# First FFN chunk in plain float32, smaller early chunks, weights divided one chunk later, clears issued behind the raw weights

## The chip, the core and the metric

The kernel runs on one core of a Trainium2 chip. A core has a matrix engine (TensorE, PE in the profile; its weight loads are PEld), three engines for elementwise work (VectorE or DVE, ScalarE or ACT, GpSimd or POOL), an engine that issues most transfers (SyncE or SP), and 16 DMA engines. Each engine works through its own instruction stream in order and waits for others by semaphores. Matrix results land in PSUM, eight banks of 512 float32 in each of 128 partitions; everything else lies in SBUF or in device memory. The metric is device time in microseconds, the median of several runs.

## The reference

Three layers follow each other: attention that keeps the 32 largest scores of each row, a feed-forward layer (FFN) with a squared ReLU, and a mixture of 8 experts of which each token uses two.

```python
scores = scale * np.matmul(q, k.transpose(0, 1, 3, 2))          # 4 x 8 x 576 x 576, head size 64
kth = np.partition(scores, -top_k, axis=-1)[..., -top_k:-top_k + 1]   # top_k = 32
scores = np.where(scores >= kth, scores, -1000000000.0)
attn = np.exp(scores - np.max(scores, axis=-1, keepdims=True))
x = (attn / (attn.sum(-1, keepdims=True) + 1e-09)) @ v          # 2304 tokens x 512
h = np.maximum(x @ w_in, 0.0); x = h * h @ w_out                # 512 -> 2048 -> 512
logits = x @ w_gate + np.log1p(np.exp(x @ w_noise)) * noise     # two largest of 8 experts
out[mask] += top2_w * (np.maximum(x[mask] @ w1[e], 0.0) @ w2[e])  # 512 -> 1024 -> 512
```

The FFN's weights arrive as 64-bit floats, the rest as float32.

## The kernel before

**Tokens.** The 2304 tokens make 18 tiles of 128. Each of the four batches has 576 queries: four full tiles and 64 left over, and the leftovers of two batches share a tile. Attention goes by units. A full unit is one tile and one pair of heads (64 of them); a left unit is 64 leftover queries and one pair of heads (16). `LEFT_AFTER` says after which tile of its batch the left units stand. In a unit TensorE multiplies queries and keys (line 394), VectorE searches the 32 largest scores (lines 407 to 448; two searches in a full unit, one in a left one, 144 in all, each with two instructions of line 435), GpSimd and ScalarE mask and exponentiate (lines 460 to 466), TensorE transposes (lines 477, 500, 501) and multiplies with the values (line 514), and `finish` divides by the row sum and splits the result (lines 486 to 492).

**Split matmuls.** Where a matmul must be as good as float32, both operands are split into a high part that the engine's fast format holds exactly and a low remainder, and three fast matmuls (high-high, high-low, low-high) are summed. The keys and queries, the FFN (lines 319 to 321 and 305 to 307) and the experts work so. Products with the values, transposes and routing logits (line 188) are plain float32.

**FFN chunks.** `CHUNKS` cuts the 18 tiles into six chunks of three. A chunk's `ffn` is a generator of small pieces. It becomes available when all units of its tiles are done. For each of 16 slices f of the hidden layer it loads the divided weights `wi` and `wo` (512 KB each, two buffers) from the scratch tensor `wsc`, does four first steps (three matmuls each, as wide as the chunk), squares the ReLU and splits it (lines 325 to 329), and does one second step a tile for the slice before (three matmuls of 512 columns). The sums of up to three tiles stand in the three banks of `ps_acc` until line 176 moves them out; then `route` picks the experts and scatters the rows to the slots `xs`.

**Conversions.** `convert` turns the 64-bit weights into divided float32, 32 pieces in all: it loads a raw piece (512 KB, three buffers), ScalarE and VectorE build the high word (lines 153, 155, 156, the scratch in PSUM for the first 14 pieces and in SBUF after), ScalarE and GpSimd add the low word (157, 158), then both split the value (161, 162), and it is written to `wsc` (163). 

**Clears.** `zero_fill` writes empty rows to the experts' slots (40 transfers of 258 KB) and to the output (18 of 256 KB).

**Order.** The program is written unit by unit. Between parts of a unit `step` takes FFN and routing pieces from the background, as many as a rate (`FIRST_RATE`, `RATE`, in estimated us a unit, less for left units) allows, and `side` takes conversions (three a unit) and, from unit 9 of the list on, clears. Each side work gets a priority, and a scheduler sets the final order on every engine by priority and its own estimate of time. Two kinds of instructions keep a fixed order among themselves by a token: the searches, and the last chunk with the early experts. After attention the rest of the FFN runs, three experts start on their first 384 slots while the last chunk finishes, and then the experts follow one another.

## Time and profile before

| | |
|---|---|
| median of 3 runs | 1365.13 us (1363.53 to 1368.26) |
| the profiled execution | 1361.43 us |
| its span, first to last instruction | 1359.7 us |
| TensorE busy | 1240.0 us, 91% |
| VectorE busy | 889.0 us, 65% |
| ScalarE busy | 862.3 us, 63% |
| GpSimd busy | 773.3 us, 57% |
| mean granted TensorE clock | 0.971 |

The shares are averages over stages with different limits, so they are to be read stage by stage. Matmuls are pipelined and their printed lengths overlap: how fast TensorE goes is read from start to start. A matmul whose operands are both plain float32 appears as two instructions. In the chain of waits a piece is the work that the end of the program was waiting for at that moment.

### The profile page before, as it was taken

What the parts mean: (1) busy time and instruction counts of PE and PEld (TensorE: products, weight loads), DVE (VectorE), ACT (ScalarE), POOL (GpSimd) and SP (SyncE); (2) the same over time, 40 slices, a digit from 0 to 9 for tenths busy, and PEclk for the clock granted to TensorE, in tenths of its full rate; (3) what the DMA queues carried; (4) which work ended last, traced back from release to release, by engine and by line L of the source; (5) the groups of instructions that cost most, each with busy time, mean ns of one, the idle gap of its engine ahead of it and who ended that gap; (6) DMA issues with size and microseconds to landing.
All of it is one profiled execution on the core that took longest, in us unless ns stands there. A gap on an engine that the chain in (4) does not pass through costs nothing.

```text
span 1359.7 us, 25767 instructions
## 1 busy us (share of the span) xinstructions
PE 1240.0 (91%) x7937; PEld 1083.3 (80%) x7937; DVE 889.0 (65%) x4531; ACT 862.3 (63%) x1849; POOL 773.3 (57%) x1239
## 2 busy tenths in 40 slices
PE   3666689889999999899999998999999999999997
PEld 2554478778887888688878887889999899899876
DVE  7999979898777888998698101255544444444554
ACT  6988888898788878988797443543433323333343
POOL 5869999867875757777656536233441331513232
PEclk9787699999999999999999999999999999999999
DMA  9996688734764356166415768645653443434464
GB/s 321 362 359 232 207 298 303 257 122 136 253 215 163 122 178 226 44 198 220 153 57 176 234 245 272 221 147 194 202 165 122 134 148 124 150 114 146 137 202 139
DMA packets 86387, 261.65 MB, mean 192 GB/s; under 512 B 10844, under 2 KB 10972, under 8 KB 86240
## 3 DMA queue, kind: packets, MB, share of 16 engines
q1 hardware_dynamic: 76960, 231.51, 51.6%
q0 software_dynamic: 9280, 28.40, 5.7%
q8 instruction: 65, 1.06, 0.3%
q14 instruction: 82, 0.67, 0.2%
HBM read 209.90 MB, written 52.06 MB: 193 GB/s over the span
## 4 chain that ended last, share of the span: by engine, by line
PE 67%; DVE 9%; DMA 7%; ACT 4%; POOL 3%; issue 2%; SPq 0%; POOLq 0%; DVEq 0%; ACTq 0%
PE ph L643 5%; PE ph L644 5%; PE ph L645 5%; PE acc L624 5%; PE acc L626 5%; PE acc L625 5%; PE pa L514 4%; PE acc L305 4%; PE acc L306 4%; PE acc L307 4%; PE ps L394 4%; PE pf L319 4%; PE pf L321 3%; PE pf L320 3%; PE pa L477 3%; DVE w L411 2%
## 5 line engine op out<-in xcount | busy, mean ns | idle before, releaser
L407 DVE MAX8 m<-sb 128x8 f32<-128x115 f32 (+1 forms) x720 | 190.4, 265 | 69.5 <-ACT sb L396 64.5
L465 POOL TENSOR_TENSOR sb<-sb,w 128x576 f32<-128x576 f32 x144 | 205.7, 1430 | 46.4 <-ACT w L464 44.0
L411 DVE MATCH_REPLACE8 w<-m,sb 128x115 f32<-128x115 f32 (+1 forms) x720 | 186.9, 262 | 0.0
L665 POOL DMA_INDIRECT out<-y,info x40 | 45.9, 1148 | 241.2 <-DVE y L664 223.5
L649 ACT ACTIVATE ht<-ph 128x384 fp32r<-128x384 f32 (+1 forms) x128 | 55.8, 436 | 194.5 <-PE ph L645 194.5
L394 PE MATMUL ps<-K,qt 128*128 128x288 f32 (+2 forms) x640 | 130.6, 333 | 43.5 <-ACT sb L396 22.3
L650 DVE SCALAR_TENSOR_TENSOR ht<-ph,ht 128x384 fp32r<-128x384 f32 (+1 forms) x128 | 62.6, 489 | 162.3 <-ACT ht L649 162.2
L643 PE MATMUL ph<-xe,wi 128*128 128x256 f32 (+1 forms) x512 | 159.4, 311 | 1.7 <-ACT wi L636 1.2
L645 PE MATMUL ph<-xe,wi 128*128 128x256 f32 (+1 forms) x512 | 158.6, 310 | 0.2 <-DVE wi L637 0.2
L644 PE MATMUL ph<-xe,wi 128*128 128x256 f32 (+1 forms) x512 | 158.7, 310 | 0.0
L394 PEld LDWEIGHTS ps<-K,qt 128*128 128x128 f32 x640 | 103.4, 204 | 59.8 <-ACT sb L396 31.7
L329 POOL TENSOR_TENSOR gt<-r,gt 128x384 fp32r<-128x384 f32 x96 | 98.1, 1023 | 73.5 <-ACT gt L328 60.1
L466 ACT ACTIVATE sb<-sb,keep 128x576 f32<-128x576 f32 x144 | 112.2, 779 | 27.9 <-POOL sb L465 27.0
L624 PE MATMUL acc<-wo,ht 128*128 128x512 f32 x320 | 125.9, 397 | 0.7 <-DVE y L664 0.7
L625 PE MATMUL acc<-wo,ht 128*128 128x512 f32 x320 | 125.2, 395 | 0.0
L319 PE MATMUL pf<-xT,wi 128*128 128x384 f32 x320 | 111.9, 350 | 10.2 <-ACT xT L491 4.7
L305 PE MATMUL acc<-wo,gt 128*128 128x512 f32 x288 | 113.7, 409 | 6.3 <-DMA wo<-wsc 5.1
L464 ACT ACTIVATE w<-sb,keep 128x576 f32<-128x576 f32 x144 | 111.4, 775 | 11.7 <-POOL keep L460 11.0
L435 DVE MAX8 m<-w 128x8 f32<-128x288 f32 x288 | 115.7, 442 | 0.1
L477 PE MATMUL pa<-ident,sb 128*128 128x128 f32 x576 | 96.8, 293 | 19.1 <-ACT sb L466 10.3
L320 PE MATMUL pf<-xT,wi 128*128 128x384 f32 x320 | 110.7, 346 | 3.5 <-POOL xT L492 3.4
L306 PE MATMUL acc<-wo,gt 128*128 128x512 f32 x288 | 111.8, 402 | 0.0
(203 smaller groups left out, 3440.5 us busy)
## 6 DMA issues: line engine op xcount, KB each, us to landing
wi<-wsc SPq DMA_DIRECT2D x96, 512.0 KB, 4.7
wo<-wsc SPq DMA_DIRECT2D x96, 512.0 KB, 4.8
raww<-in_exp SPq DMA_DIRECT2D x88, 512.0 KB, 3.7
raw<-in_ffn SPq DMA_DIRECT2D x32, 512.0 KB, 6.0
wsc<-csp SPq DMA_DIRECT2D x32, 512.0 KB, 4.5
xs<-xr SPq DMA_DIRECT2D x40, 258.0 KB, 7.2
mr<-xs SPq DMA_DIRECT2D x40, 258.0 KB, 3.1
qn<-in_q SPq DMA_DIRECT2D x40, 256.0 KB, 4.2
```

The costliest lines, as they stand in the source:

```text
L305: nc.tensor.matmul(acc[tt], gt[:, 0, sl], wo[:, 0, :], start=(f == 0), stop=False)
L306: nc.tensor.matmul(acc[tt], gt[:, 0, sl], wo[:, 1, :], start=False, stop=False)
L319: nc.tensor.matmul(ph[:, 0:n], wi[:, 0, sl], xT[:, 0, c, 0:n], start=(c == 0), stop=False)
L394: nc.tensor.matmul(ps[:, n, 0:w], st, kt[:, at:at + w], start=(i == 0), stop=(i == len(pairs) - 1))
L407: in_turn(nc.vector.max(parts[i][1], sb[:, parts[i][0]]))
L411: in_turn(nc.vector.match_replace(out=w[:, sl], in_to_replace=top, in_values=sb[:, sl], imm_value=NEG))
L465: nc.gpsimd.tensor_tensor(sb, sb, w, op=ALU.subtract)
L624: queued(nc.tensor.matmul(acc[t], hs[i][:, 0, sl], wo[:, 0, :], start=(f == 0), stop=False))
L625: queued(nc.tensor.matmul(acc[t], hs[i][:, 0, sl], wo[:, 1, :], start=False, stop=False))
L643: queued(nc.tensor.matmul(ph[:, 0:n], wi[:, 0, sl], xe[i][:, 0, c, :], start=(c == 0), stop=False))
L644: queued(nc.tensor.matmul(ph[:, 0:n], wi[:, 0, sl], xe[i][:, 1, c, :], start=False, stop=False))
L645: queued(nc.tensor.matmul(ph[:, 0:n], wi[:, 1, sl], xe[i][:, 0, c, :], start=False, stop=(c == NC - 1)))
```

## The change

- `CHUNKS` is now 2, 2, 2, 3, 3, 3, 3. The left units of the first batch stand behind its sixteen full units.
- Chunk 0 (two tiles) is computed with plain float32 matmuls, one where three stood; `finish` writes its input without a split, and the squared ReLU is not split either.
- A conversion ends with the whole value, written to a new scratch tensor `whole` (256 KB a piece). It no longer splits. Raw pieces and converted ones have four buffers each.
- Chunk 1 loads both whole pieces of a slice at once, divides them (ScalarE makes the high parts, GpSimd the low part of `wi`, VectorE that of `wo`), writes them to `wsc` and uses them. The later chunks load from `wsc` as before.
- Raw loads and clears share an issue-order token, so that no clear goes ahead of a raw load that is written earlier in the program.
- The rate of background work is worked out for each chunk from its pieces and the units until the next but one chunk is due, instead of two constants.

```diff
-CHUNKS = [3, 3, 3, 3, 3, 3]
-LEFT_AFTER = [3, 2, 0, 2]
+CHUNKS = [2, 2, 2, 3, 3, 3, 3]
+LEFT_AFTER = [4, 2, 0, 2]
...
+    def queue_turn(inst):
+        tc.stamp_issue_order_token(inst.ins, "loads")
...
-                nc.sync.dma_start(xs[e * NT + t * P:e * NT + (t + 1) * P, :], fill)
+                queue_turn(nc.sync.dma_start(xs[e * NT + t * P:e * NT + (t + 1) * P, :], fill))
...
-        nc.sync.dma_start(raw, w_ffn[f, which])
+        queue_turn(nc.sync.dma_start(raw, w_ffn[f, which]))
...
-        val = a.bitcast(F32)
-        sp = vpool.tile([P, 2, n], F32R, name="csp", bufs=2 if keep is not None else 1)
-        nc.scalar.activation(sp[:, 0, :], val, AF.Copy)
-        nc.gpsimd.tensor_tensor(sp[:, 1, :], val, sp[:, 0, :].bitcast(F32), op=ALU.subtract)
-        nc.sync.dma_start(wsc[f][:, which], sp.bitcast(F32))
+        nc.sync.dma_start(whole[f][:, which], a.bitcast(F32))
...
+        plain, divide = t0 == 0, t0 == CHUNKS[0]
...
+                if plain:
+                    nc.tensor.matmul(acc[tt], gt[:, 0, sl].bitcast(F32), wo[:, 0, :].bitcast(F32),
+                                     start=(f == 0), stop=(f == NF - 1))
...
+            if plain:
+                for i, w in enumerate((wi, wo)):
+                    nc.sync.dma_start(w[:, 0, :].bitcast(F32), whole[f][:, i])
+            elif divide:
+                raw = vpools[0].tile([P, 2 * DM], U32, name="raw", bufs=4 if keep is not None else 2).bitcast(F32)
+                nc.sync.dma_start(raw, whole[f].rearrange("p a d -> p (a d)"))
+                for i, (w, eng) in enumerate(((wi, nc.gpsimd), (wo, nc.vector))):
+                    part = raw[:, i * DM:(i + 1) * DM]
+                    nc.scalar.activation(w[:, 0, :], part, AF.Copy)
+                    eng.tensor_tensor(w[:, 1, :], part, w[:, 0, :].bitcast(F32), op=ALU.subtract)
+                    nc.sync.dma_start(wsc[f][:, i], w.bitcast(F32))
...
+                if plain:
+                    nc.tensor.matmul(ph[:, 0:n], wi[:, 0, sl].bitcast(F32), xT[:, 0, c, 0:n].bitcast(F32),
+                                     start=(c == 0), stop=(c == NC - 1))
...
+        rates.append(pieces(nt, i == 0) / sum(weight[done_at[i] + 1:until] + [1.0]))
...
-        return (FIRST_RATE if state["chunk"] == 0 else RATE) * (weight[i] if i < NU else 1.0)
+        return rates[state["chunk"]] * weight[i]
```

How the built program's order changes is shown at three places. First the transfer queue (SP) in the early program. `raw` is a raw weight piece, `xs` an empty slot block (a clear), `qn` queries. Before, around the fourth raw load:

```order
L136 DMA xs<-xr 128x516 x5
L147 DMA raw<-in_ffn 128x1024
L136 DMA xs<-xr 128x516 x4
L147 DMA raw<-in_ffn 128x1024
L136 DMA xs<-xr 128x516 x2
L163 DMA wsc<-csp 128x1024
L136 DMA xs<-xr 128x516
L163 DMA wsc<-csp 128x1024
L136 DMA xs<-xr 128x516 x2
L147 DMA raw<-in_ffn 128x1024
L136 DMA xs<-xr 128x516 x5
```

And in the changed program, from the 30th raw load on:

```order
L149 DMA raw<-in_ffn 128x1024
L138 DMA xs<-xr 128x516 x5
L161 DMA whole<-ca 128x512
L149 DMA raw<-in_ffn 128x1024
L406 DMA qn<-in_q 128x512
L161 DMA whole<-ca 128x512
L149 DMA raw<-in_ffn 128x1024
L138 DMA xs<-xr 128x516 x10
L161 DMA whole<-ca 128x512 x2
L138 DMA xs<-xr 128x516 x5
L161 DMA whole<-ca 128x512
L138 DMA xs<-xr 128x516 x6
```

Clears stood between the raw loads; now nearly all stand behind them, and the output's clears follow.

Next VectorE between two searches, marked by the pairs `MAX m<-w` at lines 435 and 462. `low` and `m` are search work; `ca` is a conversion's value. Before, from the 12th search to the 13th:

```order
L435 MAX m<-w 128x8 x2
L407 MAX m<-sb 128x8
L438 TENSOR_SCALAR low<-m 128x5x11
L411 MATCH_REPLACE w<-m,sb 128x116
L443 MAX low_868<-low 128x8
L407 MAX m<-sb 128x8
L446 MATCH_REPLACE low<-low_868,low 128x5x11
L411 MATCH_REPLACE w<-m,sb 128x115
L443 MAX low_868<-low 128x8
L407 MAX m<-sb 128x8
L446 MATCH_REPLACE low<-low_868,low 128x5x11
L411 MATCH_REPLACE w<-m,sb 128x115
```

And in the changed program, from the 12th search on:

```order
L462 MAX m<-w 128x8 x2
L434 MAX m<-sb 128x8
L158 SCALAR_TENSOR_TENSOR ca<-raw,ca 128x512
L157 TENSOR_SCALAR ca<-ca 128x512
L465 TENSOR_SCALAR low<-m 128x5x11
L438 MATCH_REPLACE w<-m,sb 128x116
L499 RECIPROCAL sm<-sm 128x2
L158 SCALAR_TENSOR_TENSOR ca<-raw,ca 128x512
L470 MAX low_823<-low 128x8
L434 MAX m<-sb 128x8
L157 TENSOR_SCALAR ca<-ca 128x512
L473 MATCH_REPLACE low<-low_823,low 128x5x11
```

Where a search stood alone, the steps of several conversions stand within it; sixteen searches into the program thirty conversions have been placed, against six before.

Last TensorE around the 11th unit, whose value matmuls are `pa<-pt,vt`. `pf` and `acc` are FFN results, the rest is attention. Before:

```order
L514 MATMUL pa<-pt,vt 64x128 x8
L477 MATMUL pa<-ident,sb 128x128 x8
L319 MATMUL pf<-xT,wi 128x384
L500 MATMUL pa<-ident,sb 128x128
L501 MATMUL pa<-ident,rb 128x128
L320 MATMUL pf<-xT,wi 128x384
L321 MATMUL pf<-xT,wi 128x384
L394 MATMUL ps<-K_120,qt 128x288 x4
L514 MATMUL pa<-t_1928,vt 64x128 x2
L514 MATMUL pa<-pt,vt 64x128 x8
```

And in the changed program:

```order
L545 MATMUL pa<-pt,vt 64x128 x8
L504 MATMUL pa<-ident,sb 128x128 x4
L338 MATMUL pf<-xT,wi 128x256 x4
L504 MATMUL pa<-ident,sb 128x128 x4
L531 MATMUL pa<-ident,sb 128x128
L532 MATMUL pa<-ident,rb 128x128
L338 MATMUL pf<-xT,wi 128x256 x4
L421 MATMUL ps<-K_258,qt 128x288 x4
L545 MATMUL pa<-t_1934,vt 64x128 x2
L545 MATMUL pa<-pt,vt 64x128 x8
```

The first single steps of chunk 0 stood there; now whole slices of the plain chunk stand there. By the counts of the whole order, TensorE had 64 first and 48 second steps (of three matmuls) ahead of unit 28's value matmuls, 312 and 231 ahead of unit 80's, and 72 and 57 after. Now it has the whole plain chunk with 52 and 22 two-tile steps ahead of unit 28, 300 first steps (128 of them two tiles wide) and 193 second steps ahead of unit 80, and 84 and 63 after.

## Rows read from the trace of the kernel before

**Rows 1.** Stretches, core 0: engines' busy us (instructions), clock, DMA share, GB/s

```profile
0.00:98.00 98.00, 54.04 (x315) 41.94 (x316) 88.19 (x527) 77.38 (x152) 69.41 (x101) 0.88 1.01 354
98.00:306.00 208.00, 165.96 (x1125) 138.23 (x1125) 192.79 (x1077) 179.47 (x397) 186.76 (x210) 0.89 0.69 236
306.00:781.00 475.00, 459.44 (x3361) 402.11 (x3358) 368.89 (x2484) 387.29 (x876) 328.29 (x522) 1.00 0.51 170
540.00:600.00 60.00, 52.89 (x406) 45.06 (x405) 57.26 (x394) 55.04 (x125) 44.53 (x76) 0.97 0.30 97
781.00:884.00 103.00, 95.41 (x506) 83.54 (x506) 13.26 (x41) 45.24 (x89) 41.92 (x99) 0.98 0.73 245
884.00:1360.00 476.00, 465.18 (x2639) 417.44 (x2637) 225.87 (x408) 172.95 (x336) 146.97 (x310) 0.99 0.47 151
```

**Rows 2.** Chain of waits, searches: start, us, engine, tile, line, count

```profile
290.86 0.72 DVE m L435 x2
294.68 0.73 DVE m L435 x2
298.71 0.72 DVE m L435 x2
```

**Rows 3.** Groups of instructions: busy us, mean ns, idle before and releaser

```profile
L637 DVE TENSOR_TENSOR wo<-raww,wo 128x512 fp32r<-128x512 f32 x88 | 60.7, 690 | 26.1 <-ACT wo L636 24.9
L162 POOL TENSOR_TENSOR csp<-ca,csp 128x512 fp32r<-128x512 f32 x32 | 42.2, 1321 | 2.9 <-ACT csp L161 2.6 <-POOL keep L460 0.3
L158 POOL TENSOR_TENSOR ca<-ca,raw 128x512 uint32<-128x512 uint32 x32 | 41.6, 1301 | 5.5 <-issue 2.7 <-POOL xT L492 0.7 <-POOL keep L460 0.7
L156 DVE SCALAR_TENSOR_TENSOR ca<-raw,ca 128x512 uint32<-128x512 uint32 x18 | 22.3, 1241 | 0.2
L155 DVE TENSOR_SCALAR ca<-ca 128x512 uint32<-128x512 uint32 x18 | 16.4, 909 | 6.9 <-ACT ca L153 6.9
L155 DVE TENSOR_SCALAR acc<-acc 128x512 uint32<-128x512 uint32 x14 | 9.6, 688 | 0.0
L156 DVE SCALAR_TENSOR_TENSOR ca<-raw,acc 128x512 uint32<-128x512 uint32 x14 | 9.4, 673 | 0.0
```

**Rows 4.** Timeline, TensorE: start, us; the value matmuls of units 8, 28, 80

```profile
98.30 0.54 PE L514 MATMUL pa<-t,vt 128*64 128x128 f32 x4
...
305.65 0.44 PE L514 MATMUL pa<-t,vt 128*64 128x128 f32 x4 [1.25 <-ACT t L503]
...
779.52 0.44 PE L514 MATMUL pa<-t,vt 128*64 128x128 f32 x4
```

**Rows 5.** Line 176: the moves out of PSUM of all chunks' sums

```profile
L176 ACT COPY xr<-acc x18: 569/592/618, 286.5 to 879.5; 128x512 f32<-128x512 f32 x18
```

**Rows 6.** Timeline, TensorE: neighbours of 384, 512 and 256 columns

```profile
809.00 0.34 PE L321 MATMUL ph<-xT,wi 128*128 128x384 f32 x1
809.17 0.34 PE L319 MATMUL ph<-xT,wi 128*128 128x384 f32 x1
...
811.23 0.39 PE L305 MATMUL acc<-wo,gt 128*128 128x512 f32 x1
811.46 0.40 PE L306 MATMUL acc<-wo,gt 128*128 128x512 f32 x1
...
1004.53 0.28 PE L643 MATMUL ph<-xe,wi 128*128 128x256 f32 x1
1004.65 0.28 PE L644 MATMUL ph<-xe,wi 128*128 128x256 f32 x1
```

**Rows 7.** Chain of waits: value matmuls, scores, plain float32 matmuls of routing

```profile
332.25 1.24 PE pa L514 x20
334.25 1.29 PE ps L394 x8
...
803.37 1.85 PE acc L188 x16
807.63 0.98 PE acc L188 x8
```

More of the change, by code (lines that the diff above doesn't have):

```diff
@@ L81, in attention_ffn_moe @@
     tag = "" if keep is not None else "x"
+    whole = [nc.dram_tensor(f"whole{tag}{f}", (P, 2, DM), F32, kind="Internal").ap() for f in range(NF)]
     wsc = [nc.dram_tensor(f"wsc{tag}{f}", (P, 2, 2, DM), F32, kind="Internal").ap() for f in range(NF)]
@@ L145, in convert @@
         n = DM
-        raw = vpool.tile([P, 2 * n], U32, name="raw", bufs=3 if keep is not None else 2)
-        nc.sync.dma_start(raw, w_ffn[f, which])
+        raw = vpool.tile([P, 2 * n], U32, name="raw", bufs=4 if keep is not None else 2)
+        queue_turn(nc.sync.dma_start(raw, w_ffn[f, which]))
         pair = raw.rearrange("p (j t) -> p j t", t=2)
         lo_w, hi_w = pair[:, :, 0], pair[:, :, 1]
-        a = vpool.tile([P, n], U32, name="ca", bufs=2)
+        a = vpool.tile([P, n], U32, name="ca", bufs=4 if keep is not None else 2)
         high = ps_acc.tile([P, DM], F32, name="acc") if 2 * f + which < IN_PSUM else a.bitcast(F32)
@@ L296, in attention_ffn_moe @@
     after, mpools = [], []
+    vpools = []
     def ffn(t0, nt, xT):
@@ L326, in ffn @@
             gt = fpool.tile([P, 2, CH], F32R, name="gt")
[L327 to L329 removed]
+            if plain:
+                nc.scalar.activation(gt[:, 0, 0:n].bitcast(F32), r[:, 0:n], AF.Square)
+            else:
+                nc.scalar.activation(r[:, 0:n], r[:, 0:n], AF.Square)
+                nc.scalar.activation(gt[:, 0, 0:n], r[:, 0:n], AF.Copy)
+                nc.gpsimd.tensor_tensor(gt[:, 1, 0:n], r[:, 0:n], gt[:, 0, 0:n].bitcast(F32), op=ALU.subtract)
             yield True, 0.163 * nt
@@ L480, in transpose4, with finish @@
         return t
-    def finish(av, rt, dst, j, off, n):
+    def finish(av, rt, dst, j, off, n, plain):
+        if plain:
+            with tc.high_priority(SOON):
+                nc.vector.tensor_tensor(dst[:, 0, j, off:off + n].bitcast(F32), av[:, 0:n], rt, op=ALU.mult)
+            return
         x = apool.tile([P, P], F32, name="x", bufs=4)
@@ L675, in attention_ffn_moe, with pieces @@
     state = {"safe": True, "due": 0.0, "chunk": 0, "routed": 0}
-    def pieces(nt):
-        return NF * (NC * nt * 0.163 + nt * 0.65)
+    def pieces(nt, plain):
+        return NF * nt * (NC * (0.2 if plain else 0.163) + (0.8 if plain else 0.65))
     def step(n):
@@ L735, in attention_ffn_moe @@
                     units.append((b, NFULL * P, False, j, tiles.index((b - b % 2, None))))
+        if LEFT_AFTER[b] == NFULL:
+            units += [(b, NFULL * P, False, j, tiles.index((b - b % 2, None))) for j in range(H // 2)]
     NU = len(units)
@@ L780, in close @@
                     nc.gpsimd.tensor_copy(dsts[ch][:, :, :, (tt - t0) * P:(tt - t0 + 1) * P], lefts[tt])
-            background.append([ffn(t0, nt, dsts[ch]), pieces(nt)])
+            background.append([ffn(t0, nt, dsts[ch]), pieces(nt, ch == 0)])
+    rates = []
+    for i, (t0, nt) in enumerate(chunks):
+        until = done_at[i + 1] if i + 1 < len(chunks) else NU
+        rates.append(pieces(nt, i == 0) / sum(weight[done_at[i] + 1:until] + [1.0]))
     def rate(i):
-        return (FIRST_RATE if state["chunk"] == 0 else RATE) * (weight[i] if i < NU else 1.0)
+        return rates[state["chunk"]] * weight[i]
     q_split(0)
```

22 lines of the change are left out of this document (12 added, 10 removed).

## Prediction

> **What bounds the kernel now.** I read the stretches of the span first, one line per stage [rows 1]. In the first 306 us VectorE is the busy engine (88.2 of 98 us, then 192.8 of 208) and TensorE is not: 166 of 208 us by a busy count that includes matmul latency, at a granted clock of 0.88 to 0.89 of 2.4 GHz, so part of the time at 1.2. From 306 to 781 us, the rest of attention, this turns round: TensorE is busy 459.4 of 475 us, VectorE 368.9. From 781 to 884 us TensorE does FFN that attention left over, and from 884 us the experts, which the change does not touch. So time is saved only by matmul work moved forward into TensorE's early idle time, and an added matmul costs its full length unless it falls there.
>
> Then the prices. A search (one of 144, two in a full unit, one in a left unit) costs VectorE 4.0 us where nothing else holds it: its L435 pairs start 3.8 and 4.0 us apart [rows 2]. A conversion costs it 0.69 + 0.67 = 1.36 us with PSUM scratch (the first 14) and 0.91 + 1.24 = 2.15 us with SBUF scratch (the other 18), GpSimd 1.30 + 1.32 = 2.62 us [rows 3]. The last matmul group of unit 8 starts at 98.3 us, of unit 28 at 305.7, of unit 80 at 779.5 [rows 4]; I use these three as milestones. Chunk 0's sums leave PSUM at 286.5 us [rows 5], close to unit 28. TensorE's steps go by start to start, not by the length printed: 0.176 us for 384 columns (two at 0.17, rounded; a run of twelve gives 0.176), 0.234 for 512, 0.118 for 256 [rows 6]. A float32 matmul is two passes of 0.109 us for 128 columns, from (1.85 - 0.98)/8 [rows 7]. A first step (three matmuls of one slice) is thus 0.527 us for three tiles and 0.354 for two, a second step (three matmuls of 512 columns) 0.703. A full unit's own TensorE work is 1.29 for scores, ten transposes at 0.109 and 1.24 for values, 3.6 us [rows 7]; a left unit's I estimate at 3.0.
>
> **The change, part by part.** *TensorE, in all.* One FFN tile in three split matmuls takes 16 x (12 x 0.176 / 3 + 3 x 0.234) = 22.5 us. In plain float32 it takes 16 x (4 x 2 x 0.109 + 8 x 0.109) = 27.9 us. Chunk 0 has two tiles: 55.8 instead of 45.0, so TensorE has 11 us more to do. Two-tile chunks cost nothing more, as 0.118 is two thirds of 0.176. Where these 11 us land decides the case, and the order of the built program says how much FFN stands before each unit. Before unit 28 stood chunk 0, 67.5 us; now 55.8 + 52 x 0.354 (first steps) + 22 x 0.703 (second steps) = 89.7. Between units 28 and 80 stood 248 x 0.527 + 183 x 0.703 = 259; now 76 x 0.354 + 172 x 0.527 + 171 x 0.703 = 238. After unit 80 stood 72 x 0.527 + 57 x 0.703 = 78; now 84 and 63, 88.6. So: **+22, -21.6, +10.5 us.**
>
> *To unit 8.* Six conversions stood before its sixteenth search, now thirty do. VectorE therefore does 8 x 1.36 + 16 x 2.15 = 45 us more before that point, and nothing hides it, since VectorE is the bound there (88 of 98 us). Unit 8 goes from 98 to 143 us. At PSUM prices for all 24 it would be 33 us more, 131 us; both ends are kept. TensorE has some 30 us of work in this time, eight units at 3.6 and a first step or two, so it idles about 113 us, against 68 before. The clears no longer stand ahead of the raw loads, so I add no stall for those.
>
> *Units 9 to 28.* VectorE: 36 searches x 4.0, two conversions (4 us), and eleven of the sixteen new wo subtractions of chunk 1 at 0.69 [rows 3], 8 us: 156 us. TensorE: 16 x 3.6 + 4 x 3.0 + 89.7 + 3 for routing = 162 us. They do not overlap perfectly. In units 13 to 20 the program gives TensorE 68 us against 48 for VectorE, because four of them are left units and two steps of chunk 0 stand in each; in the other twelve units VectorE's 108 us is longer. That makes 176 us. In the same units VectorE lost 14 us before (208 us, for 194 of searches and conversions); GpSimd, busy 187 of 208, had a part in that and is relieved, so I add half, 7 us. Unit 28 comes at 143 + 183 = 326 instead of 306: **+20 us**. The low end is 131 + 162 = 293 (-13), the high end 143 + 176 + 14 = 333 (+27). So the early start fills TensorE's idle time of this stage, after the front loading has made about as much in the stage before.
>
> *Units 29 to 80.* TensorE is the bound here and has 21.6 us less. VectorE's total, 92 x 4.0 + 3.5 = 372 of 474 us, is far from it. But in units 29 to 36 and 45 to 48 the program now leaves so little FFN that searches set the pace for a few us. I take **-19 us**. It is -22 if nothing is lost, and -9 if half these units lose 5% as 540 to 600 us does, where VectorE sets the pace and 57.3 of 60 us are busy [rows 1].
>
> *After unit 80.* **+10.5 us**, on the path: TensorE is busy 95.4 of 103 us, and the stretch ends with the last chunk's routing. If the 7.6 idle us absorb most of it, +3; if two more weight loads are waited for, +13.
>
> *At nothing:* ScalarE's and GpSimd's savings in chunk 0 (no gt split, no x split) and the division moved from conversion to chunk 1. ScalarE is busy 179 of 208 us, and its copies keep their number. If ScalarE became late in units 21 to 28, where two copies a step stand beside the searches, it would cost up to 8 us, which the high end covers.
>
> **Sum.** +20 - 19 + 10.5 = +11.5 on the profiled execution's 1361.4 us: 1372.9. The median of the runs shown is 3.7 above that execution, so about **1376 us** by the median.
>
> **A rule against a row.** L156 takes 0.67 us where one operand lies in PSUM and 1.24 where both lie in SBUF [rows 3], while GpSimd was busy almost without pause. The Trainium skill, SBUF — State Buffer, section Who interferes with whom, says that a VectorE instruction with two SBUF inputs and a GpSimd instruction that reads SBUF exclude each other, one fully blocking. By that rule the 18 late conversions get cheaper as GpSimd's part of a conversion halves. The rows agree with the rule as far as the two forms differ.
>
> **Rivals.** *Cheaper conversions: faster.* If halving GpSimd's 2.62 us per conversion takes the SBUF form down to 1.36 on VectorE, unit 8 comes at 131, and if the two engines then mesh in units 9 to 28, unit 28 at 293: -13 - 22 + 10.5 = -24.5, or 1341. Half of it (unit 28 at 303) gives 1354. It decides from unit 28 at about 311, where the sum is -4. For it: 1.24 against 0.67 in the same line. Against it: the searches between need the same GpSimd, and the two-input wo subtractions come on top. Chance 0.23.
>
> *Clears before chunk 0: slower still.* The 58 clears, 15 MB, now go out together after the last raw load. At the 354 GB/s of the first 98 us they need 42 us. In the program 38 stand ahead of the weight load of chunk 0's third step. If that is late by 15 us at unit 10, TensorE waits with units 11 and 12 queued behind it: 1390. For it: loads and clears share one queue. Against it: the first clears go while the last conversions run. Chance 0.15.
>
> *Gains and losses cancel.* Unit 28 at 315 and the leftover partly absorbed: within 0.3%, 1365. Chance 0.20. That bound of 0.3% is about what a measurement of this kernel can tell from no change.
>
> **How the numbers follow.** My forecast, slower by 5 to 20 us, has 0.42; with the clears' case, slower holds 0.57, same 0.20, faster 0.23. The likeliest time is 1376. The range goes from 1352, which leaves out the faster rival's better half, to 1393, the clears' case with a little more: together the ends leave out about 0.2.
>
> **What would show it.** Right: unit 8 near 143 us, with TensorE idle in more than two thirds of the time until then; unit 28 near 326; from there to unit 80 some 455 us instead of 474; first-chunk sums out of PSUM near 225; about 10 us more between unit 80 and the experts. Wrong: L158 (the old L156) near 0.7 us in its SBUF form, or unit 28 before 311, speaks for the faster rival; TensorE waiting for wi or wo from whole around units 10 to 12 speaks for the clears. If the experts' stretch is not 476 us again, something I have not seen is at work.

## The result, and the profile after

The changed kernel takes 1375.0 us (median of 11 runs, 1370.6 to 1376.8), the kernel before beside it 1365.1 us (11 runs, 1362.7 to 1369.6). The ratio is 1.0059 with a 95% interval of 1.0044 to 1.0074: slower by 0.6%, outside the 0.3% that the prediction called no change. The profiled execution took 1376.78 us with a span of 1375.0, that of before 1361.43 with 1359.7. So the two traces lie 15.3 us apart and the medians 9.9; the traces tell where time went, the medians how much of it is usual.

The milestones that answer to [rows 4], the value matmuls of units 8, 28 and 80, from the timeline of TensorE after the change (start, us, engine, line, operation):

```profile
132.57 0.70 PE L545 MATMUL pa<-t,vt 128*64 128x128 f32 x4
...
321.72 0.44 PE L545 MATMUL pa<-t,vt 128*64 128x128 f32 x4
...
781.24 0.44 PE L545 MATMUL pa<-t,vt 128*64 128x128 f32 x4
```

The stretches between them, and the experts after; then two slices of 20 us. Columns as in [rows 1]: length, busy us of PE, PEld, DVE, ACT and POOL with instruction counts, granted TensorE clock, DMA share, GB/s.

```profile
0.00:132.57 132.57, 64.06 (x322) 49.33 (x322) 126.00 (x565) 99.65 (x187) 95.00 (x112) 0.76 0.90 311
132.57:321.72 189.15, 175.03 (x1184) 136.79 (x1183) 165.28 (x1069) 157.94 (x371) 128.90 (x183) 0.95 0.67 234
321.72:781.24 459.52, 443.67 (x3313) 385.40 (x3313) 370.43 (x2480) 380.34 (x889) 322.49 (x519) 0.99 0.53 180
781.24:888.60 107.36, 98.70 (x529) 87.05 (x528) 10.13 (x36) 43.36 (x87) 48.78 (x104) 0.97 0.74 261
888.60:1375.00 486.40, 475.18 (x2689) 426.54 (x2687) 227.99 (x411) 178.43 (x348) 148.07 (x313) 1.00 0.46 151
...
100.00:120.00 20.00, 9.98 (x48) 7.28 (x46) 20.00 (x83) 13.03 (x27) 13.83 (x14) 0.59 0.98 309
...
200.00:220.00 20.00, 20.00 (x120) 14.74 (x119) 11.33 (x75) 13.53 (x30) 12.51 (x17) 1.00 0.53 178
```

For the same two last stretches of the kernel before, which [rows 1] cuts at other points:

```profile
779.52:873.60 94.08, 87.51 (x478) 76.84 (x477) 10.70 (x36) 39.23 (x79) 41.63 (x96) 0.98 0.77 258
873.60:1359.70 486.10, 474.56 (x2690) 425.45 (x2688) 228.49 (x411) 179.34 (x348) 148.22 (x313) 0.99 0.47 151
```

Read against [rows 1, 4], the path is **+34.3 us to unit 8, -18.2 from there to unit 28, -14.4 to unit 80, +13.3 from there to the experts, +0.3 in the experts**: 15.3. In the first stretch VectorE is busy 126.0 of 132.6 us and TensorE 64.1, at a granted clock of 0.76. In the second TensorE's idle time has fallen from 42 us to 14. There is one place where TensorE is the bound now and was not: at 200 to 220 us the plain float32 chunk keeps it busy 20.00 of 20 us while VectorE has 11.33; before, no slice of 20 us between units 8 and 28 has TensorE full.

Groups of the conversion and the division (busy us, mean ns; idle before and releaser), answering to [rows 3], and the moves of all chunks' sums out of PSUM, answering to [rows 5]:

```profile
L158 DVE SCALAR_TENSOR_TENSOR ca<-raw,ca 128x512 uint32<-128x512 uint32 x18 | 19.1, 1062 | 0.0
L157 DVE TENSOR_SCALAR ca<-ca 128x512 uint32<-128x512 uint32 x18 | 16.3, 906 | 0.0
...
L329 DVE TENSOR_TENSOR wo<-raw,wo 128x512 fp32r<-128x512 f32 x16 | 13.9, 866 | 0.0
```

```profile
L174 ACT COPY xr<-acc x18: 565/588/616, 245.5 to 894.6; 128x512 f32<-128x512 f32 x18
```

**A ledger of TensorE.** Up to the first expert matmul TensorE is busy or idle, and a busy us at a low granted clock does less. I took windows of about 4 us, some 220 per kernel, and multiplied TensorE's busy time in each by its granted clock (1.00 is the 2.4 GHz level): that is the work, and all other time is lost, to waiting or to the lower level. It is an estimate: with the coarse stretches above in place of the small windows the sums differ by up to 2 us, and the work of kernels with the same matmuls scatters by some 6 us either way.

| us | to unit 8 | 8 to 28 | 28 to 80 | 80 to experts | sum |
|---|---|---|---|---|---|
| before: lost | 52.2 | 55.7 | 16.9 | 8.3 | 133.1 |
| before: work | 46.0 | 151.6 | 457.0 | 85.8 | 740.4 |
| after: lost | 86.5 | 21.9 | 20.4 | 11.6 | 140.4 |
| after: work | 46.0 | 167.2 | 439.1 | 95.9 | 748.2 |

The time lost in the first stretch grows by 34.3 us and that in the second falls by 33.8. The conversions' move to the front and the FFN's earlier start cancel. What remains is 8 us more work and 7 us more lost, half of it between units 28 and 80 and half behind unit 80. Between units 28 and 80 nearly all of it is low clock: TensorE's busy time less its work is 1.3 us there before and 4.6 after.

### The profile page after: what moved, and what is told of

It is laid out like the page before. It is cut to its first block, busy times and chain, and to the rows that moved or that the text cites. A ratio compares the mean times of both kernels' runs of the same rounds, so it can differ in the third digit from the quotient of the medians.

```text
span 1375.0 us, 26197 instructions
## 1 busy us (share of the span) xinstructions
PE 1256.7 (91%) x8030; PEld 1085.1 (79%) x8030; DVE 899.8 (65%) x4557; ACT 859.7 (63%) x1879; POOL 743.2 (54%) x1229
## 3 DMA queue, kind: packets, MB, share of 16 engines
q8 instruction: 65, 1.06, 0.3%
## 4 chain that ended last, share of the span: by engine, by line
PE 69%; DVE 13%; ACT 8%; DMA 6%; POOL 2%; issue 2%; SPq 0%; POOLq 0%; DVEq 0%; ACTq 0%
PE ph L674 5%; PE ph L676 5%; PE ph L675 5%; PE acc L655 5%; PE acc L656 5%; PE acc L657 5%; PE pa L545 5%; PE ps L421 4%; PE acc L311 4%; PE acc L312 3%; PE acc L313 3%; PE pa L504 3%; PE pf L343 3%; PE pf L345 3%; PE pf L344 2%; DVE w L438 2%
## 5 line engine op out<-in xcount | busy, mean ns | idle before, releaser
L680 ACT ACTIVATE ht<-ph 128x384 fp32r<-128x384 f32 (+1 forms) x128 | 55.7, 435 | 194.1 <-PE ph L676 176.4
L421 PE MATMUL ps<-K,qt 128*128 128x288 f32 (+2 forms) x640 | 134.3, 339 | 36.1 <-ACT sb L423 17.9
L356 POOL TENSOR_TENSOR gt<-r,gt 128x384 fp32r<-128x384 f32 (+1 forms) x96 | 89.3, 931 | 69.8 <-ACT gt L355 62.9
L655 PE MATMUL acc<-wo,ht 128*128 128x512 f32 x320 | 125.6, 396 | 0.5 <-DVE y L695 0.5
L656 PE MATMUL acc<-wo,ht 128*128 128x512 f32 x320 | 125.2, 395 | 0.0
L343 PE MATMUL pf<-xT,wi 128*128 128x384 f32 (+1 forms) x312 | 102.7, 329 | 7.0 <-ACT r L349 3.5
L657 PE MATMUL acc<-wo,ht 128*128 128x512 f32 x320 | 108.8, 400 | 0.0
L311 PE MATMUL acc<-wo,gt 128*128 128x512 f32 x256 | 104.9, 414 | 3.7 <-ACT gt L355 1.5
L504 PEld LDWEIGHTS pa<-ident,sb 128*128 128x128 f32 x576 | 68.2, 147 | 46.8 <-issue 15.7
```

Source lines behind the costliest of these rows:

```text
L311: nc.tensor.matmul(acc[tt], gt[:, 0, sl], wo[:, 0, :], start=(f == 0), stop=False)
L421: nc.tensor.matmul(ps[:, n, 0:w], st, kt[:, at:at + w], start=(i == 0), stop=(i == len(pairs) - 1))
L504: nc.tensor.transpose(pt[:, c * P:(c + 1) * P], e[:, c * P:(c + 1) * P], ident)
L655: queued(nc.tensor.matmul(acc[t], hs[i][:, 0, sl], wo[:, 0, :], start=(f == 0), stop=False))
L656: queued(nc.tensor.matmul(acc[t], hs[i][:, 0, sl], wo[:, 1, :], start=False, stop=False))
L657: queued(nc.tensor.matmul(acc[t], hs[i][:, 1, sl], wo[:, 0, :], start=False, stop=(f == NFE - 1)))
```

## The experiments

Each ratio is to the kernel before, run beside the kernel of the row (its medians were 1362.0 to 1365.1 us). "Work" and "lost" are the sums of the ledger, up to the experts; the last column is how many tiles of FFN are in plain float32.

| kernel | median, us | ratio (95%) | unit 8 | unit 28 | unit 80 | experts | work | lost | plain |
|---|---|---|---|---|---|---|---|---|---|
| before | 1365.1 | 1 | 98.3 | 305.7 | 779.5 | 873.6 | 740.4 | 133.1 | 0 |
| after | 1375.0 | 1.0059 (1.0044 to 1.0074) | 132.6 | 321.7 | 781.2 | 888.6 | 748.2 | 140.4 | 2 |
| e1_split0 | 1385.5 | 1.0157 (1.0125 to 1.0188) | 130.1 | 316.5 | 784.1 | 897.8 | 745.4 | 152.3 | 0 |
| e2_clears | 1374.2 | 1.0089 (1.0057 to 1.0122) | 100.5 | 314.9 | 771.6 | 882.8 | 753.4 | 129.6 | 2 |
| e5_plain2 | 1393.4 | 1.0211 (1.0180 to 1.0242) | 131.6 | 325.0 | 798.4 | 901.3 | 759.4 | 141.8 | 4 |
| e6_queue_only | 1394.0 | 1.0219 (1.0188 to 1.0249) | 119.4 | 331.3 | 803.5 | 903.9 | 741.0 | 162.7 | 0 |
| e7_chunks | 1404.8 | 1.0303 (1.0273 to 1.0332) | 96.7 | 306.0 | 800.7 | 915.5 | 749.7 | 165.9 | 0 |
| e11_split0_free | 1391.8 | 1.0211 (1.0183 to 1.0239) | 100.5 | 323.6 | 787.6 | 896.2 | 744.5 | 151.7 | 0 |
| e12_one | 1382.2 | 1.0124 (1.0093 to 1.0154) | 101.3 | 321.1 | 778.6 | 894.1 | 747.1 | 147.2 | 1 |
| e10_rate | 1367.3 | 1.0024 (1.0005 to 1.0044) | 101.4 | 318.4 | 771.6 | 882.0 | 756.7 | 125.1 | 2 |
| e15_bigtok | 1414.7 | 1.0377 (1.0335 to 1.0419) | 132.5 | 328.3 | 812.3 | 924.7 | 756.6 | 168.0 | 3 |
| e16_bigrate | 1398.2 | 1.0261 (1.0229 to 1.0293) | 99.6 | 327.4 | 817.6 | 911.2 | 757.4 | 153.7 | 3 |
| e18_bigsplit | 1383.6 | 1.0152 (1.0119 to 1.0185) | 99.6 | 316.7 | 803.4 | 898.0 | 741.4 | 156.5 | 0 |
| e19_before_rate | 1372.7 | 1.0063 (1.0040 to 1.0087) | 99.3 | 310.1 | 802.7 | 880.7 | 736.6 | 144.1 | 0 |

My theory was that the plain float32 chunk is what is lost (11 us of TensorE work) and that the rest cancels. The first four runs undo or double one part each.

### e1: the plain chunk undone

```diff
-        plain, divide = t0 == 0, t0 == CHUNKS[0]
+        plain, divide = False, t0 == 0
```
(and the same flag for `finish` and `pieces`)

> The changed kernel with its first chunk in split matmuls and the division into halves moved from the second chunk to the first; everything else of the change stays. Theory (the plain float32 chunk adds TensorE work that comes back in full in the span): its eight slice pairs cost 27.9 - 22.5 = 5.4 us less per tile, 11 us for two tiles, so about 1364 us, and TensorE's busy sum from the first unit to the experts about 11 us below the changed kernel's. Rival (the chunk's extra TensorE time fills pauses that would stand there anyway, and what costs is the early converting): 1372 to 1378 us. Second rival (dividing inside the first chunk, while the conversions still run, holds chunk 0's matmuls back): slower than the changed kernel, 1380 to 1390 us.

1.0157: slower than the changed kernel by about 10 us, not faster by 11. The theory's time fell, the second rival's came. Two of its stretches, and three of TensorE's waits from 100 to 322 us, those of split FFN matmuls (who waited for whom: us in total, times, longest):

```profile
130.14:316.54 186.40, 156.58 (x1173) 131.04 (x1172) 170.50 (x1072) 160.41 (x384) 142.21 (x197) 0.94 0.77 267
...
784.12:897.80 113.68, 105.43 (x568) 92.66 (x567) 11.18 (x43) 44.89 (x90) 52.09 (x108) 0.97 0.75 261
```

```profile
PE pf L344 <- POOL xT L523: 6.0, 2, 4.6
...
PE pf L343 <- ACT r L349: 5.0, 2, 3.4
...
PE pf L345 <- POOL wi L329: 2.7, 3, 1.3
```

The same of the changed kernel: two waits of its plain matmuls, and the only one for a divided weight:

```profile
PE pf L338 <- DVE xT L512: 2.7, 2, 1.6
...
PE acc L312 <- DVE wo L329: 1.9, 2, 1.7
...
PE pf L338 <- ACT r L349: 0.8, 2, 0.5
```

Between units 8 and 28 TensorE is idle 29.8 us where the changed kernel has 14.1. Two of the waits are for low parts, which plain matmuls don't have: of the FFN's input (`xT`, 6.0 us) and of `wi` (2.7 us). The third is for ScalarE's ReLU (`r`, 5.0 us). In the changed kernel the plain matmuls wait 3.5 us in the same time, 2.7 for `xT` and 0.8 for `r`. So plain float32 is dear in work, but its operands need no split and no division, and the version without them is 10 us slower. Which of these costs it is not shown: the weights' division, the split of the input and that of the squared ReLU came back together, the waits for divided weights are about 3 us where 16 us of idle time were added, and the dividing was not tried alone.

### e5: the plain work doubled

```diff
-        plain, divide = t0 == 0, t0 == CHUNKS[0]
+        plain, divide = t0 < 4, t0 == 4
```
(and the same flag for `finish` and `pieces`)

> The changed kernel with two plain float32 chunks instead of one, the division moved to the third chunk: the same cost a second time. Theory (plain float32 is paid in full): + 2 tiles x 5.4 us = about 11 us, 1386 us, with more of it standing after unit 80 or between units 28 and 80. Rival (the plain passes fill pauses): within 4 us of the changed kernel, 1371 to 1379 us. Rival (plain chunks relieve ScalarE and GpSimd of the split, and that is worth more than the TensorE time): 1365 us or less.

1.0211, 18 us over the changed kernel by the medians, 13.6 us in the two traces. The stretches from unit 8 on:

```profile
131.56:325.01 193.45, 183.90 (x1118) 135.91 (x1117) 158.66 (x1079) 145.16 (x332) 103.82 (x159) 0.95 0.50 172
325.01:798.40 473.39, 448.14 (x3294) 385.23 (x3294) 380.95 (x2469) 388.45 (x903) 337.85 (x521) 0.99 0.54 181
798.40:901.30 102.90, 96.01 (x515) 85.13 (x515) 10.13 (x36) 43.28 (x87) 46.60 (x101) 0.97 0.77 270
```

TensorE's busy time up to the experts rises from 781.5 to 792.0 us, by 10.5; idle time by 2. Here the extra plain work is paid in full, as the theory said, but the median lies 7 us above its 1386, and the division moved one chunk further with it; what of the rest that costs is not separated. The table says the same over all kernels: the six without plain float32 besides the kernel before have 737 to 750 us of work, mean 743; one tile 747; two 748, 753, 757; three 757, 757; four 759. That is 4 to 5 us a tile, where the prediction had 5.4. The price is real in every kernel. Whether it is worth paying is another question, and e1 answers it for the first chunk.

### e2: the order of loads and clears undone

```diff
     def queue_turn(inst):
-        tc.stamp_issue_order_token(inst.ins, "loads")
+        return
```

> The changed kernel without the issue order for raw loads and clears, so the scheduler places the clears where it likes, among the raw loads: by the built order 9 instead of 30 conversions stand ahead of search 16, 30 ahead of search 32. Theory (the work is the same and only moves between stretches): unit 8 falls to 105 to 115 us, units 8 to 28 take that back, and the whole is within 0.5% of the changed kernel, 1369 to 1381 us. Rival (the ordered clears hold back the first chunk's weights): 1360 to 1366 us. Rival on the other side (without the order the raw loads come late, and the first chunk, which reads the converted weights, waits for the conversions): 1385 us and more, with TensorE's pauses at the first-chunk matmuls in units 12 to 28.

1.0089 (1.0057 to 1.0122), no difference from the changed kernel's 1.0059. The stretches:

```profile
0.00:100.49 100.49, 54.49 (x326) 42.68 (x326) 93.49 (x549) 77.20 (x149) 63.58 (x92) 0.88 1.01 359
100.49:314.93 214.44, 187.90 (x1257) 145.78 (x1257) 202.58 (x1105) 183.55 (x427) 171.63 (x216) 0.96 0.76 261
314.93:771.59 456.66, 433.59 (x3218) 372.96 (x3217) 366.25 (x2452) 376.00 (x870) 310.23 (x504) 0.99 0.50 166
771.59:882.80 111.21, 99.55 (x545) 87.45 (x545) 12.13 (x43) 43.48 (x87) 50.94 (x107) 0.97 0.76 258
882.80:1370.80 488.00, 475.22 (x2690) 426.52 (x2688) 227.84 (x411) 178.40 (x348) 147.38 (x313) 0.99 0.48 151
```

Unit 8 comes at 100.5 us, 32 us earlier than in the changed kernel, and unit 28 only 7 us earlier. So 32 us of front loading or none make no difference to the end, which is the clearest sign in this study that the early stretches only trade time. The loss of the clears' rival (weights of the first chunk held back) isn't there either way: without the order the time is the same.

### e6: the order alone, on the kernel before

```diff
-        nc.sync.dma_start(raw, w_ffn[f, which])
+        queue_turn(nc.sync.dma_start(raw, w_ffn[f, which]))
```
(and the same for both clears)

> The kernel before with only the issue order added to the raw loads and the clears (the loads first, the clears behind); chunks, conversions and division stay as before. By the built order 15 instead of 12 conversions stand ahead of search 16, and the first chunk's matmuls come later: 19 instead of 48 us of them before unit 20, 318 instead of 326 us before unit 80. Theory (order moves work, it saves none; what is not done before unit 80 is paid behind it): 8 us slower than the kernel before, 1369 to 1375 us. Rival (the order alone is a gain, and the plain chunk eats it): 1350 to 1358 us. Rival (no effect): 1362 to 1368 us.

1.0219, 30 us slower; I had expected 8. Four stretches of it:

```profile
0.00:119.43 119.43, 61.75 (x317) 47.16 (x317) 108.37 (x584) 95.88 (x189) 98.77 (x125) 0.81 0.73 254
119.43:331.32 211.89, 166.97 (x1089) 139.96 (x1088) 172.23 (x1024) 163.53 (x359) 158.09 (x189) 0.86 0.75 253
...
240.00:260.00 20.00, 10.20 (x51) 8.83 (x50) 19.20 (x133) 13.87 (x30) 12.07 (x16) 0.76 1.02 379
260.00:280.00 20.00, 20.00 (x139) 17.99 (x138) 9.34 (x60) 12.77 (x29) 10.20 (x13) 0.98 0.58 185
```

Unit 8 is 21 us later: in the trace 14 conversions stand ahead of VectorE's 16th search where the kernel before has 6 (its 12, which the expectation names, are those ahead of the 24th). Unlike in the changed kernel the second stretch does not give it back: it takes 211.9 us where the kernel before takes 207.4. From 220 to 240 us no FFN matmul starts; at 240 to 260 TensorE is busy 10.20 us while VectorE has 19.20; right behind, at 260 to 280, TensorE has 20.00 and VectorE 9.34. The same FFN pieces stand in other places: first hardly any, then too many. The work is that of the kernel before (741.0), 30 us more are lost.

### e7: the chunk sizes with their planner rates, on the kernel before

```diff
-CHUNKS = [3, 3, 3, 3, 3, 3]
+CHUNKS = [2, 2, 2, 3, 3, 3, 3]
```
(with the new planner rates and the leftover tiles' new place)

> The kernel before with the chunk sizes 2, 2, 2, 3, 3, 3, 3, their planner rates and the leftover tiles' place alone: conversions write both halves as before, no plain float32, no issue order on loads and clears, the old buffer counts. Theory (the 15 us by which the changed kernel's experts start later, in the profiled pair, are its 11 us of plain float32 and some 4 us of low granted clock, and its earlier start is worth nothing): work as before, 765 us of TensorE up to the experts, idle about 108 us, 1360 to 1368 us. Rival (the earlier start of the FFN is a gain, and the plain chunk eats it): idle of TensorE under 100 us, 1350 to 1358 us. Rival (small chunks late in coming leave TensorE idle, since the built order has 51 instead of 68 us of FFN ahead of unit 28 and 311 instead of 326 ahead of unit 80): 1372 to 1380 us.

1.0303, 41 us slower, more than any of the three expectations. It is not the sizes alone: by the planner's own code its rates are 5.21, 4.01, 4.01, 4.34, 5.21 and 6.01 for the first six chunks, where the kernel before has 5.5 and then 6.0, so most units take less FFN with them. Sizes and rates were not tried apart. Stretches, and one wait of TensorE from 100 to 322 us:

```profile
96.70:306.00 209.30, 152.84 (x1088) 123.69 (x1087) 192.41 (x1081) 174.97 (x399) 180.53 (x210) 0.90 0.72 245
306.00:800.72 494.72, 471.39 (x3463) 407.89 (x3462) 366.64 (x2481) 396.01 (x915) 326.10 (x539) 0.99 0.55 181
800.72:915.50 114.78, 104.83 (x568) 92.25 (x567) 11.19 (x43) 44.99 (x90) 52.14 (x108) 0.97 0.75 259
```

```profile
PE pf L347 <- DMA wi<-wsc: 13.2, 8, 5.7
```

The first chunk starts while the conversions still run (in the trace 6 of them stand ahead of the 16th search and 17 ahead of the 32nd, where the kernel before has 6 and 19). The FFN's matmuls wait for `wi` eight times, 13.2 us, and TensorE idles 56.5 us between units 8 and 28 against 42. The FFN that is not done there is done late: unit 80 and the experts come 21 and 42 us later.

### e11 and e12: two mixtures

e11 is e2 and e1 together; e12 is e2 with chunks of 1, 3, 2, 3, 3, 3, 3 tiles.

> The changed kernel without the issue order and without the plain chunk (first chunk in split matmuls, divided there). Theory, from the two single steps (without the order 1374 us; without the plain chunk 1386 us, where TensorE's work fell by 11 us but pauses and low clock grew by 20 us): the pauses come from dividing ahead of each of the first chunk's slices, and without the order the conversions are spread out and cost less of the early stretch: 1366 to 1374 us. Rival (the loss is in the dividing itself, whatever the order): 1380 to 1390 us.

> The changed kernel without the issue order, with chunks of 1, 3, 2, 3, 3, 3, 3 tiles: only one tile in plain float32, the division in a chunk of three. Theory (plain float32 costs 5.4 us a tile and is paid in full): TensorE's busy sum up to the experts 5 us under the two-tile version's 775.5 us, 1366 to 1371 us. Rival (one tile is too little to fill the early pauses; the second chunk comes late): idle grows by more than 5 us, 1375 to 1385 us.

e11 gives 1.0211: without the order, too, the plain first chunk beats the split one, by 17 us (e2: 1374.2). It was expected at 1366 to 1374; the time lies at the rival's end. A split first chunk of two tiles, divided there, loses with the order and without it. Waits for the divided weights are again a small part: 4.4 us between units 8 and 28, of 49 idle where e2 has 27. e12 gives 1.0124, its rival's time: by the ledger one plain tile saves 6 us of work against e2 and loses 18 us more to waiting and low clock.

### e10: higher rates

```diff
-        return rates[state["chunk"]] * weight[i]
+        return 1.15 * rates[state["chunk"]] * weight[i]
```
(on e2)

> The changed kernel without the issue order, with all planner rates of the FFN 1.15 times as high: by the built order 330 instead of 325 us of FFN matmuls ahead of unit 80. Theory (order moves work from one place to another; TensorE's idle time between units 28 and 80 falls by what is pulled ahead): 1370 to 1376 us, no difference from the same kernel at the old rates. Rival (the 23 us of idle time in that stretch stand there for lack of FFN work, 8 us more than in the kernel before): 1363 to 1368 us.

1.0024 (1.0005 to 1.0044), 7 us better than e2: the rival's time. From unit 28 on, and one group of matmuls that e2 has behind its first expert matmul and e10 has not:

```profile
318.36:771.58 453.22, 433.24 (x3260) 376.74 (x3259) 366.67 (x2480) 377.88 (x875) 317.26 (x511) 1.00 0.53 174
771.58:882.00 110.42, 100.57 (x535) 86.95 (x534) 12.94 (x38) 46.40 (x91) 45.72 (x101) 0.98 0.76 249
882.00:1365.70 483.70, 472.06 (x2671) 424.33 (x2669) 227.05 (x410) 175.14 (x342) 146.63 (x310) 0.99 0.47 149
```

```profile
L311 PE MATMUL acc<-wo,gt 128*128 128x512 f32 x6 | 2.4, 404 | 0.3 <-DMA wo<-wsc 0.3
```

Unit 80 comes at 771.6 us in both and the experts at 882.0 against 882.8. The traces differ in the experts' stretch, 483.7 us against 488.0, but that is a matter of where the mark stands: e2 has six second steps of the last chunk behind it (lines 311 to 313, 18 matmuls of 512 columns, 4.2 us at 0.234), and e10 has them ahead of it. So the gain lies before the experts. Between units 28 and 80 TensorE is idle 20.0 us where e2 has 23.1, which bears out the rival's reason for 3 of the 5 us by which the traces differ; the rest stays open.

### e15: the chunk sizes undone within the change

```diff
-CHUNKS = [2, 2, 2, 3, 3, 3, 3]
+CHUNKS = [3, 3, 3, 3, 3, 3]
```
(and the leftover tiles' old place; the planner works out other rates from these sizes)

> The changed kernel with the old chunk sizes, six chunks of three tiles, and the leftover tiles' old places; the first chunk stays plain (three tiles now), the division stays in the second, the order of loads and clears stays. The small chunks alone cost the kernel before 41 us, nearly all of it TensorE time without work (idle 133 instead of 108 us up to the experts) and low clock. Theory (a first chunk of two tiles starts before its weights are there; the plain chunk and the lighter conversion are what makes up for it): with the old sizes the waits of the first chunk go, the plain work rises by 5 us, in all 1362 to 1372 us. Rival (with light conversions the small chunks cost nothing any more, and one more plain tile costs 5 us): 1378 to 1384 us.

1.0377, 40 us slower than the changed kernel. My second theory (small chunks are the loss, the rest mends it) fell, and so did its rival. Two slices and the third stretch:

```profile
220.00:240.00 20.00, 20.00 (x103) 12.26 (x102) 8.27 (x55) 9.29 (x22) 7.22 (x11) 1.00 0.44 137
...
320.00:340.00 20.00, 16.41 (x99) 13.41 (x99) 19.08 (x135) 16.33 (x37) 13.81 (x21) 0.76 0.16 54
...
328.34:812.34 484.00, 459.38 (x3277) 397.48 (x3276) 393.91 (x2538) 395.29 (x903) 341.34 (x529) 0.98 0.50 166
```

At 220 to 240 us TensorE has 20.00 of 20 us and VectorE 8.27; this goes on from 180 to 280 us, three plain tiles in the time of eight units. At 320 to 340 VectorE has 19.08, TensorE has 16.41 at a granted clock of 0.76, because hardly any FFN stands there: 0, 2.4 and 7.2 us of FFN matmuls in the three slices from 280 to 340 us, summed from the timeline. And much of the second chunk's division now lies in the third stretch (its GpSimd subtractions run to 443 us, in the changed kernel to 329), where VectorE has 393.9 us instead of 370.4. So the small sizes with their rates, which cost 41 us on the kernel before, are worth 40 us beside the other edits, and the third plain tile has a part in that.

### e16, e18, e19: looking for a faster version

e16 is e15 without the order and with rates 1.15 times as high; e18 is e16 with a split first chunk, divided there; e19 is the kernel before with `RATE = 6.6`.

> The changed kernel with the old chunk sizes of three tiles, without the order of loads and clears, and with planner rates 1.15 times as high (347 us of FFN matmuls ahead of unit 80 by the built order instead of 325 to 330). Theory (sizes and order each cost a little, the higher rates take away some 6 us of idle time): 1355 to 1363 us, faster than both kernels. Rival (the third plain tile is paid in full, 16 us more work than the kernel before, and nothing is left to fill): 1366 to 1376 us.

> As the run before it, but with the first chunk in split matmuls, its weights divided there: no plain float32 at all, the conversions still without their two dividing steps. Theory (dividing ahead of each slice of the first chunk holds its matmuls back, whatever the chunk size: 116 to 118 us of idle time in both versions that did so, and 35 us lost to low clock): 1372 to 1385 us. Rival (it was the small first chunk that came too early; a chunk of three tiles hides the dividing, and 11 to 16 us of plain work are saved): 1345 to 1358 us.

> The kernel before with one number changed: the FFN's planner rate 6.6 instead of 6.0, as the run with higher rates pointed to (7 us less than the same kernel at the old rates, 1367 us). By the built order 338 instead of 326 us of FFN matmuls stand ahead of unit 80. Theory (FFN work pulled ahead fills TensorE's waits between units 28 and 80, 16 us of which the kernel before still has there, and behind unit 80, 7 us): 1355 to 1361 us, faster than both kernels. Rival (those waits are answers that come late whatever stands behind them, and the seven came from elsewhere): 1362 to 1369 us.

None beats the kernel before: 1.0261, 1.0152, 1.0063. e18 came where the theory had it, e16 and e19 slower than either of their expectations had it. Between e16 and e18 three plain tiles, with the division one chunk later, cost 15 us, so what is a gain for two tiles is a loss for three. e19 is the plainest case. Its stretches from unit 8 to the experts:

```profile
99.33:310.07 210.74, 169.26 (x1117) 141.44 (x1117) 192.84 (x1069) 178.91 (x397) 187.04 (x210) 0.87 0.68 232
310.07:802.68 492.61, 473.25 (x3400) 412.95 (x3400) 371.32 (x2486) 391.51 (x888) 330.91 (x527) 0.99 0.50 170
802.68:880.70 78.02, 72.48 (x398) 63.08 (x399) 10.32 (x35) 31.86 (x67) 37.32 (x89) 0.98 0.75 260
```

Beside [rows 4] and the row of before shown above, the stretch from unit 28 to 80 takes 18.7 us more and the one behind it 16.1 less, 4.2 of them because 21 FFN matmuls more now stand behind the first expert matmul. FFN that is pulled forward into a stretch where TensorE is the bound already moves and saves nothing. Lost time rises by 11 us, about half of it between units 8 and 28 and half between 28 and 80; why is not shown.

## Why the prediction was right

The time, 1375.0, is 1 us from the forecast of 1376, and the trace bears out all five stretches in sign: a later unit 8, part of it won back by unit 28, less from there to unit 80, a longer tail, unchanged experts. That it is 1 us is luck: unit 8 came 11 us earlier against the kernel before than forecast, the three stretches behind it lost 7, 5 and 3 us against theirs, so the traces lie 15.3 us apart where the sum said 11.5; and the median lies 1.8 us below the profiled execution after the change where it lay 3.7 above it before, so the medians lie 9.9 apart.

- **To unit 8: +34.3, not +45.** The low end was 131 us, and it came at 132.6. The 24 conversions were right (8 by 98.3 us before, all 32 by 132.6 after). But 18 of them took 0.91 + 1.06 = 1.97 us where 2.15 was reckoned, with 6 at 1.37 that is 44 us; one search fewer (18 against 19 by unit 8) takes 4 off; and VectorE, busy 37.5 us more, used up 3 us of idle time that the prediction had left standing. One sign failed: TensorE was to be idle in more than two thirds of this time and is idle in 68.5 of 132.6 us, 52%, because its work there is 46 us by the ledger, in both kernels, and not 30. The sum doesn't use that figure.
- **Units 9 to 28: 189 us, not 183**, so unit 28 came at 321.7 for 326. In units 13 to 20 TensorE sets the pace, as predicted from the order: 80 us there, and a slice with TensorE at 20.00 and VectorE at 11.33. The first chunk's sums left PSUM at 245.5 us, not near 225, with unit 20 at 248.
- **Units 29 to 80: 459.5, -14.4 for -19.** The work there fell by 18 us by the ledger, and 3.5 us more were lost, nearly all to low clock, for which the prediction had no term.
- **After unit 80: +13.3 for +10.5**, at the upper end that was given.
- **Plain float32, 11 us for two tiles:** TensorE's busy time up to the experts rose by 16 us, of which the ledger makes 8 work and 8 low clock, and over all kernels a tile costs 4 to 5 us. The term was right in kind and a little large.
- **The division in chunk 1, "at nothing":** right as far as TensorE goes, which waits 1.9 us for a divided weight in the whole trace. VectorE's share, which the prediction did count, was 0.87 us a subtraction of `wo` on the mean and not 0.69.
- **What the prediction had too simple: the plain chunk as pure cost.** e1 and e11 show that with split matmuls and the division in the first chunk the same kernel is 10 to 18 us slower. The forecast did not need this, since both parts were in the change.
- **Cheaper conversions** decided at unit 28 before 311; it came at 322. The form did get cheaper, 1.24 to 1.06 us, 0.18 us of the 0.79 that this rival needed. The last section shows why it was so little: what held it up was mostly GpSimd's other work, which the change does not halve.
- **Clears before chunk 0:** no wait for a weight load from `whole` among TensorE's waits there, and e2 shows no loss without the order.

The granted clock also fell in the first stretch, from 0.88 to 0.76. VectorE is busy nearly all of that time, so I take it to cost little of its own there; no run shows it.

What stays open: a price for each part alone. The order costs 30 us on the kernel before and nothing in the changed one; the sizes with their rates cost 41 us on the kernel before and are worth 40 in the change; the plain chunk, with the division behind it, is worth 10 to 18 us with two tiles and costs 15 with three. No run undoes the planner's rates, the lighter conversion or the fourth buffers by themselves, and no run takes the 10 us back whole: the nearest, e10, still stands at 1.0024. The rows show the common form of the loss, slices of 20 us in which one engine is full and the other half empty, in turn. That this imbalance is the whole cause is argued from them, not shown by a run that changes it alone.

## What to carry to other kernels

When two engines alternate as the bound, cut the span at units of work, and write down for each stretch how much the moved work adds and what idle time it removes: front loading and an earlier start are one trade, and 32 us at unit 8 were worth nothing at the end. Undo each part of a compound change before calling one of them the cost, because here the two that were tried on the kernel before, the order and the sizes with their rates, were each dearer than all parts together. Work that fills waits is only worth something in a stretch where its engine waits; pulled forward into a full one it just changes place.

## What the runs showed of the hardware

The same VectorE instruction, a two-operand combination of 128x512 values that all lie in SBUF, lasts from 0.67 to 3.03 us in the kernel before (count; minimum, median and maximum in ns; first and last start):

```profile
L156 DVE SCALAR_TENSOR_TENSOR ca<-raw,ca x18: 668/806/3026, 134.6 to 266.0; 128x512 uint32<-128x512 uint32 x18
```

and in the changed kernel:

```profile
L158 DVE SCALAR_TENSOR_TENSOR ca<-raw,ca x18: 661/1007/1573, 67.8 to 125.6; 128x512 uint32<-128x512 uint32 x18
```

The shortest are as short as the form with a PSUM operand (0.67 us, [rows 3]), in both kernels, so SBUF operands are not slower in themselves. What decides is which GpSimd instruction runs at the moment of the start. One short and one long instruction of the changed kernel with the GpSimd instruction beside the long one (start, us), then the longest of the kernel before:

```profile
74.17 0.68 DVE L158 SCALAR_TENSOR_TENSOR ca<-raw,ca 128x512 uint32<-128x512 uint32 x1
...
79.64 1.59 POOL L492 TENSOR_TENSOR sb<-sb,w 128x576 f32<-128x576 f32 x1
...
80.20 1.57 DVE L158 SCALAR_TENSOR_TENSOR ca<-raw,ca 128x512 uint32<-128x512 uint32 x1
```

```profile
194.60 5.42 POOL L357 TENSOR_TENSOR K<-kn,K 64x1152 fp32r<-64x1152 f32 x2
...
197.54 3.03 DVE L156 SCALAR_TENSOR_TENSOR ca<-raw,ca 128x512 uint32<-128x512 uint32 x1
```

At 74.17 GpSimd has nothing in hand. At 80.20 it has been masking scores (line 492) for 0.56 us, and VectorE's instruction ends 0.54 us after GpSimd's, at 81.77. At 197.54 GpSimd is in the second of two key splits (line 357), which ends at 200.02, and VectorE ends at 200.57. All 18 of the changed kernel are of these two kinds: nine start while a GpSimd instruction with two inputs runs, last 1.34 to 1.57 us and end 0.54 to 0.56 us after it; the other nine start while none runs and last 0.66 to 0.68. So the mean of 1.06 is the share of unlucky starts, and few of them meet a conversion's own GpSimd step: three of the nine, while the other six meet a mask. In the kernel before ten of the 18 took over 0.75 us, and only two of these met a conversion's step. The longest fell from 3.03 to 1.57 us because none of the 18 meets a key split any more. The Trainium skill, SBUF — State Buffer, section Who interferes with whom, says that such a VectorE instruction and a GpSimd instruction that reads SBUF exclude each other, one fully blocking. The trace agrees: an instruction that takes 0.67 us with nothing in its way ends 0.55 us behind the GpSimd instruction that it met.

TensorE's granted clock followed its pauses: 0.59 at 100 to 120 us in the changed kernel, with 9.98 of 20 us busy, and 1.00 where it had 20.00. In e7 split matmuls of 256 columns start every 0.12 us at 1.00 and every 0.21 at 0.50, behind a wait of 5.66 us for `wi`, so a pause was paid a second time in the matmuls that followed it.
